# Loads issued further ahead of their use, and P1 of the next superblock between P5 and P3

## The chip, the cores and the metric

The kernel runs on one core of a Trainium2 chip. The metric is the device time of one execution in microseconds (us), less is better. Five engines work side by side, each through its own queue of instructions in order: PE (matmuls; its weight loads are shown as PEld), DVE (VectorE), ACT (ScalarE), POOL (GpSimd) and SP (SyncE, which here issues every DMA). An engine that waits for a semaphore holds up all that stands behind in its queue.

## What is computed

```python
def _attn_ref(q, k, v, g_norm):            # 8 batches, 8 heads, 576 tokens, head 64
    kv = np.einsum('bhsd,bhse->bhde', k, v)
    out = np.einsum('bhsd,bhde->bhse', q, kv)
    rms = np.sqrt(np.mean(out * out, axis=-1, keepdims=True) + 1e-06)
    return (out / rms * g_norm).astype(np.float32)

def _moe_ref(x, w_in, w_out):              # 4608 tokens, 512 -> 2048 -> 512
    h = x @ w_in
    g = np.maximum(0.01 * h, h)
    return (g @ w_out).astype(np.float32)

def _moe2_ref(x, w_in, w_out):             # the same sizes
    h = x @ w_in
    g = h - np.tanh(h)
    return (g @ w_out).astype(np.float32)

x = attention, heads side by side, one row for each of the 8 * 576 tokens
x = _moe_ref(x, moe_w_in, moe_w_out)
return _moe2_ref(x, moe2_w_in, moe2_w_out)
```

The weights of both layers come as 64-bit floats.

## The kernel before

**Products.** A matrix product is made by Strassen's scheme with seven products P1 to P7 of half-size blocks (the table `PROD`, the class `Blocks`). Each operand block is split into a high and a low fp16 part, and `three` (L483) makes three matmuls for each product of two blocks. The left or right operand comes in two tiles: `opa` holds the three blocks that are sums by themselves, `ops` four more. `left_stages` (L420) makes them: ACT writes the high part (L429, L431), DVE the low part (L436, L438), POOL and DVE make the sums (L468). The results of the products lie in PSUM banks: P1, P6 and P7 accumulate one after the other in bank a, P2 has b, P4 has d, P5 and then P3 have c. ACT copies bank a out (`c1` after P1, `u2` after P6, `u3` after P7: the tiles `c` and `u`, L523 to L527), and DVE adds those to the others (`add`, L531, L536 to L542): block 11 after P2, 21 after P7, 22 after P5, 12 after P3. Since P3 accumulates on bank c, it may only start when 22 has been added:

```python
            need = {6: "c1", 7: "u2", 3: "22"}.get(p)
```

**Stages.** (1) To about 105 us: attention of the first batch, conversion of the first weight. (2) up1, to 595 us: `up` makes h of the first layer in 8 superblocks (one batch each, T1 = 2 x 288 tokens), each of 8 units with seven products of 6 matmuls; an activation follows and the unit `g` goes to DRAM. Between the products stand the matmuls of the attention of the next batch (`between1`). (3) down1, to 942 us: `down` multiplies g by w_out, 8 superblocks of 336 matmuls; the result x (`xst`) goes to DRAM. (4) up2, to 1305 us: 9 superblocks of T2 = 2 x 256 tokens, with tanh. (5) down2, to the end: 9 superblocks.

**A superblock of up1.** Its x is the attention of one batch. When the norms of a batch are there, DVE takes the reciprocals (L856), SP stores them (`iv`, L859), SP loads them again spread over 64 partitions (`bc`, four loads for each half kk, L867), POOL multiplies (`xg`, L874), and `left_stages` makes the operands. All that has to be done before the first product of the next superblock. Meanwhile SP also issues the loads of k, v and q of later batches (L751), the words of weights to convert (L302), the units of converted weights to split (L390) and the stores of g (L606).

**A superblock of down.** `produce` loads the eight units of g (`gl`) and makes their operands, j = 0 to 7. `superblock` then runs P1, P2 (two token halves t each), P4 by j, P6, P7, P5, P3. Each product takes all eight units, 48 matmuls for both halves.

**What sets the order.** `Plan` is a list of events by planned time. Each step has a planned duration; a chain of steps gives (engine, duration, function) tuples, where an engine None with a duration is a lead: the function (a load) is called at once and the next step is planned so much later. PE's products follow each other by `plan.on_pe`, and `plan.pe` is the planned time of the next one. Events are written out in the order of planned times, and that is the order in each engine's queue on the chip. The planned times bind nothing else. The leads are:

```python
plan.chain(t, [(None, 4.5, load), (None, 0.0, room)] + stages + [(None, 0.0, store)])
more.append([(None, 5.0, lambda kk=kk: load(kk)), ("G", 2.7, lambda kk=kk: scale(kk))] + stages)
plan.chain(t + 3.5 * kk, [(None, 5.0, load)] + stages)
```

in this order: unit of a weight (`split_late`, L403), `bc` (L883), and x for a superblock of up2 (`x1g`, in `x1_operands`, L1111). `between2` calls `x1_operands` for the next superblock of up2, `start_t` calls it for superblock 0 in the last superblock of down1. The weights `w` of a layer are loaded whole (L415) as soon as the last superblock of the layer before has used the tile (`freed`).

**Places.** L, M and X are pools of 20, 11 and 13 tiles in SBUF (`Slots`): L the large ones (g, gl, bc, x1g, ops, words), M the tiles opa and unit, X the tiles c and u of `Blocks`.

Of the kernel before, what the change touches and what calls it, by code (L numbers as in the profile page):

```python
# [130 lines left out]
def body(ctx, tc, q, k, v, g_norm, w1, w2, w3, w4, out):  # L131
# [12 lines left out]
    NL, NM, NX = 20, 11, 13  # L144
# [237 lines left out]
    def split_late(n, i, kk, t, place):  # L382
# [20 lines left out]
        plan.chain(t, [(None, 4.5, load), (None, 0.0, room)] + stages + [(None, 0.0, store)])  # L403
# [236 lines left out]

    def down(blk, T, NS, mats, width, place, ready, start_of, freed, scales=None, scale=None):
# [34 lines left out]
        def superblock(s):  # L676
            t0 = plan.pe
            start_of(s, t0)
            if s + 1 < NS:
                produce(s + 1, t0 + 1.0)  # L680
            dur = mm(width)
            for t in range(2):
                sc = scales(s) if scales else (None, None)
                bk[s, t] = Blocks(
                    dict(a=t, b=2 + 3 * t, c=3 + 3 * t, d=4 + 3 * t), width, place(s, t), None, None, ready(s, t)
                )
                bk[s, t].now = {}
                if scales:
                    def late(s=s, t=t):
                        bk[s, t].scale, bk[s, t].minus = scales(s)  # L690
                    at(t0, late)

            def whole(p, t, js=range(NP)):
# [6 lines left out]
            early = range(NP - 2) if s == 0 else range(0)  # L700
            late = range(len(early), NP)
            for p in (1, 2):
                for t in range(2):
                    if early:
                        whole(p, t, early)
            for p in (1, 2):
                for t in range(2):
                    whole(p, t, late)
            for j in range(NP):
                for t in range(2):  # L710
                    e = whole(4, t, [j])
                give("A", j, e)
            for p in (6, 7):
                for t in range(2):
                    whole(p, t)
            for t in range(2):
                whole(5, t)
            for t in range(2):
                e = whole(3, t, range(2))
            for j in range(2):  # L720
# [3 lines left out]
            for j in range(2, NP):  # L724
                for t in range(2):
                    e = whole(3, t, [j])
                give("S", j, e)
                if s == NS - 1:
                    freed(j, e)
# [113 lines left out]
    def norms(b, e):  # L843
# [35 lines left out]
        for kk in range(2):  # L879
# [3 lines left out]
            more.append([(None, 5.0, lambda kk=kk: load(kk)), ("G", 2.7, lambda kk=kk: scale(kk))] + stages)  # L883
# [55 lines left out]
    def split_all():  # L939
        for n, (i, kk) in enumerate(UNITS):  # L940
            what = ("w", 0, i - 2, 1) if i >= 2 else "s_w1"
            when(what, plan.now + 0.3 + 2.5 * n, lambda i=i, kk=kk: plan.chain(plan.now, split_first(i, kk)))
# [28 lines left out]
    for (b, c), n0 in sorted(pos.items(), key=lambda x: x[1]):  # L971
# [6 lines left out]
        else:  # L978
            for (dur, fn, after), o in zip(pair(b, c, held), OFFS):
                extra.setdefault(n0 + o, []).append((dur, fn, after))  # L980
            loads.append((n0 - 9, b, c, held))
# [28 lines left out]

    spread(lambda i, kk, t: convert(1, i, kk, t, 6.0), UNITS, START + 52.0, START + 180.0)
    spread(lambda i, kk, t: split_late(1, i, kk, t, M), UNITS, START + 200.0, end1 - 60.0)
    spread(lambda i, kk, t: convert(2, i, kk, t, 6.0), UNITS, START + 182.0, end1 - 60.0)

# [80 lines left out]
    def x1_operands(s, t):  # L1095

        x1ops[s] = [{}, {}]
        for kk in range(2):
# [21 lines left out]
            plan.chain(t + 3.5 * kk, [(None, 5.0, load)] + stages)  # L1120
# [43 lines left out]
    spread(lambda i, kk, t: convert(3, i, kk, t, 6.0), UNITS, end2 - 45.0, c3)  # L1164
    e = c3 + 18.0
    scaled[3] = [lambda: [down_scales(state[x]) for x in ("whole", "rest")]]
    spread(lambda i, kk, t: split_late(3, i, kk, t, M), UNITS, e + 1.0, end3 - 55.0)
# [73 lines left out]
```

## Time and profile before

| | us |
|---|---|
| median of 3 runs (1645.23 to 1646.91) | 1646.12 |
| the profiled execution, whole | 1649.15 |
| its span in the profile | 1647.4 |
| PE busy | 1512.3 (92%) |
| DVE busy | 1301.6 (79%) |
| ACT busy | 867.2 (53%) |
| POOL busy | 746.0 (45%) |

The profile is of one execution, so differences are made against 1649.15, and the result is then compared with the median. Times in the trace count from the start of the span. A row of a timeline tells when a run of like instructions starts on an engine and how long it lasts, and in brackets how long the engine was idle before it and what ended that. PEclk is the granted TensorE clock as a share of full speed.

### The profile page before, as it was taken

To read this page: it belongs to the slowest core of one execution; us is meant where nothing else is said; L and a number is where in the kernel's file an instruction comes from. 1 tells how busy PE (TensorE), PEld (TensorE's weight loads), DVE (VectorE), ACT (ScalarE), POOL (GpSimd) and SP (SyncE) were. 2 spreads that over 40 slices of the span, in tenths; PEclk is the share of its full clock that TensorE was granted. 3 is DMA by queue.
4 is the path that set the end of the run, shared out by engine and by line. 5 is a ranking of instruction groups with operands and counts; after the bars stand their busy time and mean duration, and the time that the engine had idled before them with its cause. 6 is when DMAs were issued, how large, how long until landed. Compare 5 with 4: busy or idle time off the path is not lost. (4 is left out here: it accounts for less than half of the span.)

```text
span 1647.4 us, 32120 instructions
## 1 busy us (share of the span) xinstructions
PE 1512.3 (92%) x12274; PEld 1227.4 (75%) x12274; DVE 1301.6 (79%) x2113; ACT 867.2 (53%) x1381; POOL 746.0 (45%) x758
## 2 busy tenths in 40 slices
PE   5299898898989999999999979999999889999998
PEld 3156675666767777777777768888888778888887
DVE  4765676576667778889989669999999988888881
ACT  3366454465655664444444246666776645455441
POOL 0356203144143345666656134446887654444440
PEclk8589999999999999999999989999999999999999
DMA  9856897898896885545455565555666844444441
GB/s 210 172 88 160 227 239 208 245 245 235 252 259 209 282 318 168 185 145 200 155 172 173 184 233 206 186 210 196 243 240 243 316 143 143 157 129 135 145 132 33
DMA packets 251578, 322.08 MB, mean 196 GB/s; under 512 B 129440, under 2 KB 194080, under 8 KB 251424
## 3 DMA queue, kind: packets, MB, share of 16 engines
q1 hardware_dynamic: 251424, 320.03, 62.7%
q8 instruction: 96, 1.57, 0.4%
q14 instruction: 58, 0.48, 0.1%
HBM read 190.84 MB, written 129.12 MB: 194 GB/s over the span
## 5 line engine op out<-in xcount | busy, mean ns | idle before, releaser
L489 PEld LDWEIGHTS <-w 128*128 128x128 f16 x8400 | 824.8, 99 | 280.1 <-issue 98.7
L468 POOL TENSOR_TENSOR gl<-gl 128x256 f32<-128x256 f32 (+1 forms) x272 | 309.5, 1138 | 307.2 <-issue 79.9
L489 PE MATMUL ps_c<-ops,w 128*128 128x288 f16 (+1 forms) x2400 | 337.3, 285 | 40.2 <-DVE g L536 28.2
L489 PE MATMUL ps_a<-ops,w 128*128 128x288 f16 (+1 forms) x2400 | 333.6, 284 | 22.2 <-ACT u L527 10.3
L489 PEld LDWEIGHTS <-ops 128*128 128x128 f16 x1728 | 169.8, 98 | 28.8 <-issue 7.7
L372 POOL TENSOR_TENSOR unit<-unit 128x128 f32<-128x128 f32 x192 | 134.1, 699 | 116.0 <-DVE wo L365 97.4
L489 PE MATMUL ps_b<-opa,w 128*128 128x288 f16 (+1 forms) x1200 | 170.2, 287 | 0.0
L489 PE MATMUL ps_a<-opa,w 128*128 128x288 f16 (+1 forms) x1200 | 166.8, 283 | 2.9 <-DMA w<-wd 2.8
L489 PE MATMUL ps_d<-opa,w 128*128 128x288 f16 (+1 forms) x1200 | 165.9, 282 | 2.7 <-DVE g L536 2.7
L468 DVE TENSOR_TENSOR gl<-gl 128x256 f32<-128x256 f32 (+1 forms) x272 | 156.0, 576 | 3.3
L874 POOL TENSOR_TENSOR xg<-xg,bc 128x1152 f32<-128x1152 f32 x16 | 43.1, 2694 | 254.3 <-DMA bc<-iv 208.7
L1145 POOL TENSOR_TENSOR g<-g,th 128x512 f32<-128x512 f32 x72 | 101.0, 1403 | 95.9 <-ACT th L1142 95.7
L431 ACT ACTIVATE ops<-gl,inv 128x1024 f16<-128x1024 f32 x72 | 82.6, 1147 | 110.2 <-POOL gl L468 102.9
L489 PEld LDWEIGHTS <-opa 128*128 128x128 f16 x1296 | 126.8, 98 | 16.6 <-issue 1.9
L429 ACT ACTIVATE ops<-gl 128x1152 f16<-128x1152 f32 x64 | 74.3, 1162 | 99.5 <-POOL gl L468 94.6
L438 DVE SCALAR_TENSOR_TENSOR ops<-gl,inv,ops 128x1024 f16<-128x1024 f32 x72 | 104.4, 1451 | 15.8 <-ACT ops L431 15.4
L436 DVE TENSOR_TENSOR ops<-gl,ops 128x1152 f16<-128x1152 f32 x64 | 99.8, 1559 | 19.9 <-ACT ops L429 19.7
L365 DVE SCALAR_TENSOR_TENSOR wo<-unit,s_w,wo 128x384 f16<-128x384 f32 (+1 forms) x96 | 83.4, 871 | 27.1 <-ACT wo L362 26.7
L489 PE MATMUL ps_c<-w,ops 128*128 128x256 f16 x864 | 98.4, 275 | 3.8 <-DVE osb L536 3.8
L489 PE MATMUL ps_a<-w,ops 128*128 128x256 f16 x864 | 96.1, 273 | 3.2 <-ACT u L527 3.2
L468 POOL TENSOR_TENSOR x1g<-x1g 128x256 f32<-128x256 f32 x72 | 68.1, 946 | 65.1 <-DMA x1g<-x 34.7
L438 DVE SCALAR_TENSOR_TENSOR opa<-gl,inv,opa 128x768 f16<-128x768 f32 x72 | 87.2, 1211 | 12.5 <-ACT opa L431 12.5
(118 smaller groups left out, 2192.3 us busy)
## 6 DMA issues: line engine op xcount, KB each, us to landing
g<-g SPq DMA_DIRECT2D x64, 576.0 KB, 4.4
gl<-g SPq DMA_DIRECT2D x64, 576.0 KB, 4.7
g<-g SPq DMA_DIRECT2D x72, 512.0 KB, 3.0
gl<-g SPq DMA_DIRECT2D x72, 512.0 KB, 4.5
wd<-wo SPq DMA_DIRECT2D x48, 448.0 KB, 2.8
w<-wd SPq DMA_DIRECT2D x24, 896.0 KB, 7.4
words<-in_moe_w_in_dram SPq DMA_DIRECT2D x64, 256.0 KB, 5.0
words<-in_moe_w_out_dram SPq DMA_DIRECT2D x64, 256.0 KB, 4.0
```

The source lines that it names most:

```text
L365: nc.vector.scalar_tensor_tensor(out=dst()[:, 1, a:b], in0=cols(0, n), scalar=scale(), in1=dst()[:, 0, a:b], op0=ALU.mult, op1=ALU.subtract,)
L372: nc.gpsimd.tensor_tensor(out=o, in0=a, in1=b, op=ALU.subtract)
L429: nc.scalar.activation(out=o, in_=i_, func=AF.Copy)
L431: nc.scalar.activation(out=o, in_=i_, func=AF.Identity, scale=scale())
L436: nc.vector.tensor_tensor(out=o, in0=i_, in1=h, op=ALU.subtract)
L438: nc.vector.scalar_tensor_tensor(out=o, in0=i_, scalar=scale(), in1=h, op0=ALU.mult, op1=ALU.subtract)
L468: lambda: e.tensor_tensor(out=g()[:, o], in0=g()[:, a], in1=g()[:, b], op=op),
L489: nc.tensor.matmul(out=out_, lhsT=a, rhs=c, start=start and m == 0, stop=stop and m == n - 1, skip_group_check=not fresh,)
L874: nc.gpsimd.tensor_tensor(out=x, in0=x, in1=held[kk].ap, op=ALU.mult)
L1145: e.tensor_tensor(out=g()[:, n], in0=g()[:, n], in1=held["t"].ap[:, n], op=ALU.subtract)
```

## The change

Six things change; the computation stays.

1. **Leads in up1.** Unit of a weight 4.5 to 9.0, words (`convert`) 6 to 13 with the start 7 earlier, `bc` 5 to 6; the loads of k, v and q stand four places earlier among the products (`n0 - 13`); conversion and splitting of late weights end 15 earlier.
2. **x of up2.** Lead of `x1g` 5 to 10; the call in `between2` at 12 before the planned PE time in place of 1 after, that in `start_t` 15 earlier.
3. **`down`.** P2 and P4 take turns by j; P1 of the next superblock stands between P5 and P3 and takes its two halves in turn; `produce` is called 6.8 (`AHEAD`) before P2 in place of 1.0 after the start of P1. Superblock 0 has P1 and P2 at its start, as before.
4. **Pools.** L 20 to 22, X 13 to 8.
5. **split_all** starts its units in pairs.
6. **split_late of the last weight** takes its tiles from L in place of M.

```diff
@@ pools @@
-    NL, NM, NX = 20, 11, 13
+    NL, NM, NX = 22, 11, 8
@@ split_late @@
-        plan.chain(t, [(None, 4.5, load), (None, 0.0, room)] + stages + [(None, 0.0, store)])
+        plan.chain(t, [(None, 9.0, load), (None, 0.0, room)] + stages + [(None, 0.0, store)])
@@ down @@
-        def superblock(s):
-            t0 = plan.pe
-            start_of(s, t0)
-            if s + 1 < NS:
-                produce(s + 1, t0 + 1.0)
-            dur = mm(width)
+        dur = mm(width)
+        one = 2 * NP * 3 * dur
+
+        def blocks(s):
...
-            for p in (1, 2):
-                for t in range(2):
-                    whole(p, t, late)
-            for j in range(NP):
-                for t in range(2):
-                    e = whole(4, t, [j])
-                give("A", j, e)
-            for p in (6, 7):
+            def in_turn(ps, s=s, then=None):
+                for j in range(NP):
+                    for p in ps:
+                        for t in range(2):
+                            e = whole(p, t, [j], s)
+                    if then:
+                        then(j, e)
+
+            start_of(s, plan.pe)
+            if s == 0:
+                blocks(0)
+                for js in (range(NP - 2), range(NP - 2, NP)):
+                    for p in (1, 2):
+                        for t in range(2):
+                            whole(p, t, js)
+            if s + 1 < NS:
+                produce(s + 1, plan.pe - AHEAD - (one if s == 0 else 0.0))
+            in_turn((4,) if s == 0 else (2, 4), then=lambda j, e: give("A", j, e))
+            for p in (6, 7, 5):
                 for t in range(2):
                     whole(p, t)
-            for t in range(2):
-                whole(5, t)
-            for t in range(2):
-                e = whole(3, t, range(2))
...
+            if s + 1 < NS:
+                blocks(s + 1)
+                in_turn((1,), s + 1)
...
+            in_turn((3,), then=end)
@@ operands of up1, attention, weights @@
-            more.append([(None, 5.0, lambda kk=kk: load(kk)), ("G", 2.7, lambda kk=kk: scale(kk))] + stages)
+            more.append([(None, 6.0, lambda kk=kk: load(kk)), ("G", 2.7, lambda kk=kk: scale(kk))] + stages)
-            loads.append((n0 - 9, b, c, held))
+            loads.append((n0 - 13, b, c, held))
-    spread(lambda i, kk, t: convert(1, i, kk, t, 6.0), UNITS, START + 52.0, START + 180.0)
-    spread(lambda i, kk, t: split_late(1, i, kk, t, M), UNITS, START + 200.0, end1 - 60.0)
-    spread(lambda i, kk, t: convert(2, i, kk, t, 6.0), UNITS, START + 182.0, end1 - 60.0)
+    spread(lambda i, kk, t: convert(1, i, kk, t, 13.0), UNITS, START + 45.0, START + 173.0)
+    spread(lambda i, kk, t: split_late(1, i, kk, t, M), UNITS, START + 200.0, end1 - 75.0)
+    spread(lambda i, kk, t: convert(2, i, kk, t, 13.0), UNITS, START + 175.0, end1 - 75.0)
@@ x of up2 @@
-            plan.chain(t + 3.5 * kk, [(None, 5.0, load)] + stages)
+            plan.chain(t + 3.5 * kk, [(None, 10.0, load)] + stages)
-            state["whole"] = second_scales(0, whole, t0 + 9.0)
-            x1_operands(0, t0 + 17.0)
+            state["whole"] = second_scales(0, whole, t0 + 5.0)
+            x1_operands(0, t0 + 2.0)
-            x1_operands(n // (NOP * NP) + 1, plan.pe + 1.0)
+            x1_operands(n // (NOP * NP) + 1, plan.pe - 12.0)
```

How this moves instructions, at three places. On SP, around the store of the norms of the fifth batch (`iv_73`) in up1, before:

```order
L606 DMA g_2_6_131<-g 128x1152
L347 DMA wf_0_0_261<-unit 128x512
L751 DMA k<-in_k_dram 96x6x64 x2
L751 DMA v<-in_v_dram 96x6x64 x2
L751 DMA q<-in_q_dram 96x6x64 x2
L302 DMA words<-in_moe_w_in_dram 128x2x256 x2
L859 DMA iv_73<-iv 16x288
L606 DMA g_2_7_132<-g 128x1152
L867 DMA bc<-iv_73 64x2x288 x4
L390 DMA unit<-wf_0_0_245 128x512
L867 DMA bc<-iv_73 64x2x288 x4
```

The same stretch in the changed kernel:

```order
L302 DMA words<-in_moe_w_in_dram 128x2x256 x2
L606 DMA g_2_6_131<-g 128x1152
L754 DMA k<-in_k_dram 96x6x64 x2
L754 DMA v<-in_v_dram 96x6x64 x2
L754 DMA q<-in_q_dram 96x6x64 x2
L347 DMA wf_0_0_261<-unit 128x512
L862 DMA iv_73<-iv 16x288
L606 DMA g_2_7_132<-g 128x1152
L870 DMA bc<-iv_73 64x2x288 x4
L390 DMA unit<-wf_0_0_245 128x512
L870 DMA bc<-iv_73 64x2x288 x4
```

The loads of k, v and q, and one pair of words, no longer stand right ahead of `iv_73` but further up, with a store of `wf` between; the `bc` loads stand behind it as they did.

On DVE, in the third superblock of down1, from the subtraction in block 21 of the second half (`xst<-u`, `ps_d`) to what follows the two adds of block 22 (`xst<-ps_c`; `u_8110` and `u_8149` are the first and the second half of the tokens), before:

```order
L540 TENSOR_TENSOR xst<-u_8149,ps_d 128x288
L894 TENSOR_REDUCE mx_322<-xst 128x1
L468 TENSOR_TENSOR gl<-gl 128x288
L894 TENSOR_REDUCE mx_322<-xst 128x1
L468 TENSOR_TENSOR gl<-gl 128x288
L542 TENSOR_TENSOR xst<-ps_c,u_8110 128x288
L436 TENSOR_TENSOR ops<-gl,ops 128x1152
L436 TENSOR_TENSOR opa<-gl,opa 128x864
L542 TENSOR_TENSOR xst<-ps_c,u_8149 128x288
L365 SCALAR_TENSOR_TENSOR wo<-unit,s_w_5985,wo 128x384
```

The same stretch in the changed kernel:

```order
L540 TENSOR_TENSOR xst<-u_8153,ps_d 128x288
L436 TENSOR_TENSOR ops<-gl,ops 128x1152
L468 TENSOR_TENSOR gl<-gl 128x288
L542 TENSOR_TENSOR xst<-ps_c,u_8112 128x288
L365 SCALAR_TENSOR_TENSOR wo<-unit,s_w_5923,wo 128x512
L436 TENSOR_TENSOR opa<-gl,opa 128x864
L897 TENSOR_REDUCE mx_322<-xst 128x1
L542 TENSOR_TENSOR xst<-ps_c,u_8153 128x288
L897 TENSOR_REDUCE mx_322<-xst 128x1
L468 TENSOR_TENSOR gl<-gl 128x288
```

Between the two adds stand a weight split, an operand split and a maximum, where there were two operand splits. On PE the 48 matmuls of P1 stand between those of P5 and P3 now.

On SP, at the start of up2, the loads of x for its second superblock (`x1g`) and of the weights (`w`), before:

```order
L415 DMA w_3_10819<-wd_3_304 128x3584
L415 DMA w_4_10829<-wd_4_305 128x3584
L415 DMA w_5_10838<-wd_5_306 128x3584
L415 DMA w_6_10846<-wd_6_307 128x3584
L415 DMA w_7_10873<-wd_7_308 128x3584
L1111 DMA x1g<-x_0_0_77 128x64
L1111 DMA x1g<-x_0_1_78 128x448
```

The same stretch in the changed kernel:

```order
L1118 DMA x1g<-x_0_0_77 128x64
L1118 DMA x1g<-x_0_1_78 128x448
L1118 DMA x1g<-x_2_0_93 128x64
L1118 DMA x1g<-x_2_1_94 128x448
L302 DMA words<-in_moe_w_out_dram 128x2x256 x2
L1042 DMA x_1_7_92<-xst 128x288
L1118 DMA x1g<-x_1_0_85 128x64
L1118 DMA x1g<-x_1_1_86 128x448
L1118 DMA x1g<-x_3_0_101 128x64
L1118 DMA x1g<-x_3_1_102 128x448
L1042 DMA x_2_7_100<-xst 128x288
L415 DMA w_0_10800<-wd_0_301 128x3584
```

The eight `x1g` loads have moved from behind the eight `w` loads to ahead of them, in two groups around the store of `x_1_7`.

## Rows read from the trace of the kernel before

**Rows 1.** Windows by stage: length, busy PE PEld DVE ACT POOL (instructions), PEclk, DMA share, GB/s.

```profile
105.30:594.80 489.50, 454.47 (x3362) 336.50 (x3361) 331.25 (x640) 278.95 (x533) 160.52 (x185) 0.96 0.80 232
594.80:942.00 347.20, 331.76 (x2654) 261.40 (x2652) 302.08 (x429) 156.58 (x203) 195.87 (x185) 0.99 0.53 177
...
975.00:1305.00 330.00, 320.30 (x2898) 283.18 (x2897) 317.81 (x531) 225.76 (x360) 208.79 (x206) 1.00 0.64 225
...
1349.00:1647.40 298.40, 294.23 (x2690) 262.78 (x2687) 230.95 (x293) 132.65 (x160) 119.98 (x114) 1.00 0.40 125
```

**Rows 2.** Timeline, fourth stop of up1: start, duration, instruction, [idle before, releaser].

```profile
308.30 1.34 DVE L856 RECIPROCAL iv<-iv 16x96 f32<-16x96 f32 x2
...
313.74 0.53 SPq L859 DMA_DIRECT2D iv<-iv  x1
...
317.40 2.58 SPq L867 DMA_DIRECT2D bc<-iv  x4
...
320.66 2.52 SPq L867 DMA_DIRECT2D bc<-iv  x4
...
326.81 2.69 POOL L874 TENSOR_TENSOR xg<-xg,bc 128x1152 f32<-128x1152 f32 x1 [0.53 <-DVE wo L365]
...
331.10 1.60 PE L489 MATMUL ps_c<-ops,w 128*128 128x288 f16 x6 [4.54 <-DVE g L536]
```

**Rows 3.** Timeline of ACT, second stop of up1.

```profile
194.56 0.67 ACT L314 ACTIVATE unit<-words 128x512 f32<-128x512 f32 x1 [8.20 <-DMA words<-in_moe_w_out_dram]
```

**Rows 4.** Down1: waits of PE and DVE (total, times, longest), windows, timelines.

```profile
PE ps_c L489 <- DVE xst L542: 11.9, 8, 2.8
...
DVE ops L436 <- ACT ops L429: 12.8, 13, 1.9
...
636.45:678.90 42.45, 41.31 (x338) 32.87 (x336) 38.94 (x53) 21.01 (x27) 27.35 (x25) 1.00 0.53 174
...
sum 262.91, PE 251.42 PEld 198.60 DVE 238.99 ACT 124.90 POOL 164.59; mean PE 41.90 PEld 33.10 DVE 39.83 ACT 20.82 POOL 27.43
...
676.35 1.05 DVE L436 TENSOR_TENSOR opa<-gl,opa 128x864 f16<-128x864 f32 x1
...
715.74 1.64 DVE L436 TENSOR_TENSOR opa<-gl,opa 128x864 f16<-128x864 f32 x1
...
717.80 6.98 PE L489 MATMUL ps_c<-ops,w 128*128 128x288 f16 x42 [2.72 <-DVE xst L542]
```

**Rows 5.** Windows of 10 us behind two stops, columns as in rows 1.

```profile
717.80:727.80 10.00, 10.00 (x68) 7.34 (x68) 8.16 (x14) 3.42 (x5) 5.30 (x6) 0.83 0.59 204
...
961.80:971.80 10.00, 9.97 (x66) 7.85 (x66) 7.60 (x23) 6.90 (x10) 4.64 (x5) 0.71 0.16 47
```

**Rows 6.** Timeline of SP, ACT and PE, start of up2.

```profile
931.11 0.33 SPq L1035 DMA_DIRECT2D x<-xst  x1
...
938.52 3.85 SPq L415 DMA_DIRECT2D w<-wd  x6
944.26 5.28 SPq L1111 DMA_DIRECT2D x1g<-x  x4
...
960.48 0.93 ACT L431 ACTIVATE opa<-x1g,s_x 128x768 f16<-128x768 f32 x1 [12.82 <-DMA x1g<-x]
...
961.83 1.44 PE L489 MATMUL ps_a<-ops,w 128*128 128x256 f16 x6 [10.33 <-ACT u L527]
```

**Rows 7.** Timeline of PE and DVE, start of down2.

```profile
1342.73 6.41 PE L489 MATMUL ps_c<-w,ops 128*128 128x256 f16 x42 [2.86 <-DVE osb L536]
1348.98 5.40 PE L489 MATMUL ps_a<-w,opa 128*128 128x256 f16 x48
...
1349.98 1.01 DVE L438 SCALAR_TENSOR_TENSOR opa<-gl,inv,opa 128x768 f16<-128x768 f32 x1
```

**Rows 8.** DMA issues: count, KB each, median us from issue to landing.

```profile
bc<-iv SPq DMA_DIRECT2D x64, 144.0 KB, 4.4
...
iv<-iv SPq DMA_DIRECT2D x8, 18.0 KB, 3.4
```

More of the change, by code (lines that the diff above doesn't have):

```diff
@@ L638, in up @@
                 count += 1
+    AHEAD = 6.8
     def down(blk, T, NS, mats, width, place, ready, start_of, freed, scales=None, scale=None):
@@ L674, in work_ @@
             return plan.on_pe(3 * len(js) * dur, go)
-        def superblock(s):
-            t0 = plan.pe
-            start_of(s, t0)
-            if s + 1 < NS:
-                produce(s + 1, t0 + 1.0)
-            dur = mm(width)
+        dur = mm(width)
+        one = 2 * NP * 3 * dur
+        def blocks(s):
             for t in range(2):
-                sc = scales(s) if scales else (None, None)
                 bk[s, t] = Blocks(
@@ L690, in late, with superblock, whole @@
                         bk[s, t].scale, bk[s, t].minus = scales(s)
-                    at(t0, late)
-            def whole(p, t, js=range(NP)):
+                    at(plan.pe, late)
+        def superblock(s):
+            def whole(p, t, js=range(NP), s=s):
                 e = work_(s, p, t, js, dur)
@@ L698, in give, with end @@
                 at(e, lambda: (M if kind == "A" else L).give(ops[s, j][kind]))
-            early = range(NP - 2) if s == 0 else range(0)
-            late = range(len(early), NP)
-            for p in (1, 2):
-                for t in range(2):
-                    if early:
-                        whole(p, t, early)
-            for p in (1, 2):
-                for t in range(2):
-                    whole(p, t, late)
-            for j in range(NP):
-                for t in range(2):
-                    e = whole(4, t, [j])
-                give("A", j, e)
-            for p in (6, 7):
+            def in_turn(ps, s=s, then=None):
[16 more added lines that the diff above has]
+            for p in (6, 7, 5):
                 for t in range(2):
                     whole(p, t)
-            for t in range(2):
-                whole(5, t)
-            for t in range(2):
-                e = whole(3, t, range(2))
-            for j in range(2):
+            if s + 1 < NS:
+                blocks(s + 1)
+                in_turn((1,), s + 1)
+            def end(j, e):
                 give("S", j, e)
@@ L723, in superblock @@
                     freed(j, e)
[L724 to L729, printed above, removed]
+            in_turn((3,), then=end)
         return produce, superblock, span
@@ L939, in split_all, with pair_ @@
     def split_all():
-        for n, (i, kk) in enumerate(UNITS):
+        def pair_(i):
+            for kk in range(2):
+                plan.chain(plan.now + 2.5 * kk, split_first(i, kk))
+        for i in range(NP):
             what = ("w", 0, i - 2, 1) if i >= 2 else "s_w1"
-            when(what, plan.now + 0.3 + 2.5 * n, lambda i=i, kk=kk: plan.chain(plan.now, split_first(i, kk)))
+            when(what, plan.now + 0.3 + 5.0 * i, lambda i=i: pair_(i))
     scaled[0] = [split_all]
@@ L1163, in body @@
     c3 = end2 + 0.45 * (end3 - end2)
-    spread(lambda i, kk, t: convert(3, i, kk, t, 6.0), UNITS, end2 - 45.0, c3)
+    spread(lambda i, kk, t: convert(3, i, kk, t, 13.0), UNITS, end2 - 45.0, c3)
     e = c3 + 18.0
     scaled[3] = [lambda: [down_scales(state[x]) for x in ("whole", "rest")]]
-    spread(lambda i, kk, t: split_late(3, i, kk, t, M), UNITS, e + 1.0, end3 - 55.0)
+    spread(lambda i, kk, t: split_late(3, i, kk, t, L), UNITS, e + 1.0, end3 - 55.0)
     out_view = out.rearrange("(b p c) d -> b c p d", p=CP, c=NC)
```

## The prediction

> **What bounds the kernel now.** I read the stages first [rows 1]. PE is the engine that is nearly always busy: 454.47 of 489.50 us in the first up stage (up1), 331.76 of 347.20 in the first down stage (down1), 320.30 of 330.00 in the bulk of up2, 294.23 of 298.40 in the bulk of down2. What a change can win without taking away matmuls is therefore PE's idle time and the time that PE runs at the lower clock. In up1 that is 489.50 - 454.47 = 35.0 us idle, and a mean granted clock of 0.96, which over 454 us of busy time is about 0.04 x 454 = 18 us. In down1 it is 15.4 us idle at 0.99. In bulk down2 it is 4.2 us, in bulk up2 9.7 us, and there DVE is busy for 317.81 of 330.00 us, so DVE is the second bound.
>
> Then I looked for what ends the idle times, one stage at a time.
>
> In up1 PE stops about once in each superblock. At the fourth stop [rows 2] the chain reads backwards like this: PE waits 4.54 us at 331.10 for a block that DVE writes; DVE and ACT stand behind the splitting of the next x operand; that waits for POOL's scaling `xg`, whose second half starts at 326.81; POOL waits for the broadcast `bc`, whose loads SP issues at 317.40 and 320.66; these need the stored norms `iv`, issued at 313.74, though the last reciprocal was done at 308.30 + 1.34 = 309.64. Four us of that are lost on SP, behind the loads of k, v and q (and one pair of words), which the order of SP before shows right ahead of the `iv` store. A second kind of stop is that ACT itself waits in its queue for a load: 8.20 us for the words of a weight at 194.56 [rows 3].
>
> In down1 PE waits eight times, 11.9 us in all, for the DVE add `xst` between P5 and P3 [rows 4]: P3 accumulates into the bank that P5 filled, and DVE has to add from it first. At 717.80 this costs 2.72 us; DVE was held by an operand split, 1.64 us at 715.74. After it the clock is 0.83 for 10 us [rows 5], 1.7 us more.
>
> At the start of up2 PE waits 10.33 us at 961.83 [rows 6]: ACT, which keeps the banks of the first superblock, stands in its queue behind the split of the second superblock's operand, and that waits 12.82 us for `x1g`, whose loads SP issues at 944.26, behind six weight loads at 938.52. At the start of down2 one wait of 2.86 us at 1342.73 [rows 7] is again P5 to P3.
>
> **Part 1, loads of up1: 24 us saved.** The stop at each superblock is set by how late the second half of `xg` starts. The code plans it 1.8 + 3.0 + 5.0 = 9.8 us after the last reciprocal, and 10.8 with the new lead of 6. In [rows 2] it came at 326.81 - 309.64 = 17.2, so 7.4 late. The change moves k, v and q four places up, out of the stretch between reciprocal and store, so the 4 us on SP go. What is left is a chain that no lead shortens, since it starts at the reciprocal: `iv` issue 0.53 and landing 3.4, four `bc` issues 2.58, a unit load 0.59, three quarters of the next 2.52, and 4.4 until the last has landed (medians of landing in [rows 8]). The sum is 0.5 + 3.4 + 2.6 + 0.6 + 1.9 + 4.4 = 13.4, still 2.6 after the plan. I take 2.5 us of stop for each of six superblocks, 15, and 4 us for what has other causes: 19 us idle in place of 35, 16 saved. A stop of that size costs 1.7 us of clock (the nearest in size is that of 2.72 us in down1, with 0.83 for 10 us after it, [rows 4, 5]), six of them 10 in place of 18: 8 saved. Together 24. The words and units, loaded 7 and 4.5 us earlier, cover ACT's 8.20 of [rows 3], which is inside the 16. The ends: if transfers stay as late as now, because the queue is as full with other loads, only ACT's wait goes, 6 us; if the chain no longer holds PE, 31 idle and 16 of clock go, 47. If earlier loads only push `bc` back further, 6 us are lost, which is the worst that I count.
>
> The Trainium skill, "SBUF — State Buffer", section "The DMA setup-cost knee", gives a transfer some 2 us plus its bytes at 436 GB/s. That is an estimate of 2.0 us for the 18 KB of `iv` and 2.3 for 144 KB; the trace has 3.4 and 4.4. With the page's figures the chain would be 9.9 and there would be no stop, which is the second case below.
>
> **Part 2, the order in down1: 12 us saved.** The matmuls are the same ones. P1 of the next superblock (48 matmuls, 5.9 us at 41.3 us of PE for 336, [rows 4]) now lies between P5 and P3, so that DVE has 5.9 us more for the add. The longest wait was 2.8, so all eight go: 11.9, and 2 x 1.7 of clock after the two longest, 15.3 at most. What is late next is the eighth operand of P1. Before, at 678.90, it was written at 676.35 + 1.05 = 677.40, and PE asked for it 7/8 x 2.9 us into P1, at 681.5: 4.1 us to spare. Now P1 stands 5.9 us earlier, but takes both halves in turn, so that its eighth part comes 5.1 us in: 3.3 earlier than before. The operands are begun 6.8 us before P2 where it was 1.0 after the start of P1, that is 1.9 earlier. So 4.1 - 3.3 + 1.9 = 2.7 us are left. The other end is DVE. In six superblocks of 262.91 us together it is busy for 238.99 and waits 12.8 for ACT's halves [rows 4], so it needs up to (239.0 + 12.8) / 6 = 42.0 us each, against 43.8 now and 41.3 of PE. If those waits stay, DVE sets the superblock, and seven of them give 7 x 1.8 = 12.6. I take 12. The upper end is the 15; for the lower, one split more in each superblock that takes 1.64 in place of 1.05 us [rows 4] leaves 7 x 1.2 = 8, and I go to 7.
>
> **Part 3, start of up2: 12 us saved.** These loads of `x1g` are now planned 13 us earlier (12 before the superblock in place of 1 after its start), and on SP it stands ahead of all weight loads, its last loads just behind the store of `x_1_7`, which was issued at 931.11. So it comes some 944.3 - 932 = 12 us earlier, and the 10.33 us of PE go; the clock after it (0.71 for 10 us, [rows 5]) gives 2.9: 13.2 at most. I keep back 1 for the weights, which now stand behind those 5.28 us of issues, while P1 of the first unit needs the first of them. Lower bound 6, if the 5.28 and its clock, 7 in all, come back.
>
> **Part 4, start of down2: 0.** The 2.86 us of [rows 7] and 1.7 of clock go, 4.6. But here the eighth operand of the next P1 was written at 1349.98 + 1.01 = 1350.99, with P1 at 1348.98 asking for it 2.3 us in, 0.3 to spare. P1 now comes 5.3 earlier for the order (48 matmuls in 5.4 us with the last one's end, [rows 7]) and 2.9 for the removed wait, and asks 2.3 later within itself: 5.9 earlier, for operands that are begun 2.6 earlier, with 0.3 to spare. A new wait of up to 3.0, with 1.7 of clock, takes the place: 4.7 lost for 4.6 won, so 0, between -4 and +4 for a DVE that is that much ahead or behind.
>
> **Part 5, the rest: 0.** Bulk down2 has PE busy for all but 4.2 us [rows 1]; there the new order finds nothing to fill. Bulk up2 is held by DVE, and its own operands, begun 13 us earlier, change nothing for DVE. Eight places for intermediates instead of thirteen could make ACT wait for an add; no row shows that. One late tile in each of 16 superblocks, by one DVE split of 1.64 us [rows 4], would be 26; I take 0, because a superblock's intermediates come free at many operations and not at one, and let the upper end of the range hold some of it. Two more places in L take nothing.
>
> **Sum.** 24 + 12 + 12 + 0 + 0 = 48 us. The profiled execution took 1649.15 us, of which the span is 1647.4; it is 3.0 over the median of 1646.12. From the median: 1646.1 - 48 = 1598.
>
> **The rivals.** *The chain of norms vanishes.* If landings in the loosened queue are as short as their best, part 1 is 47: 47 + 12 + 12 = 71, so 1575. For it: the DMA share of 0.80 in up1 [rows 1] includes what is now moved. Against: moving loads forward takes no byte out.
>
> *The queue stays as it is, and DVE holds down1.* Part 1 gives 6, part 2 gives 8, part 3 gives 12: 26, so 1620. For it: the DMA share of 0.80 over the whole stage, and DVE at 302.08 of 347.20 us in down1 [rows 1]. The second half of this has a shown cause: the same split takes 1.05 us at 676.35 and 1.64 us at 715.74 [rows 4]. The Trainium skill, "SBUF — State Buffer", section "Who interferes with whom", says that a DVE instruction with two SBUF inputs contends with a GpSimd instruction that reads SBUF; if POOL's work moves against DVE's, DVE would be the bound in all of down1.
>
> *Slower: the early P1 waits for its own operands.* P1 crosses over in 7 places of down1 and 8 of down2. With only 2.7 us to spare in the one and less than none at the first of the other, a DVE that comes 5.2 us later than before would make PE wait 2.5 at each, plus 1.7 for the clock: 15 x 4.2 = 63 us. With parts 1 and 3 standing, 36, that is 27 more than before, 1673. It decides where a crossing costs 36 / 15 = 2.4 us, a wait of 0.7 with its 1.7 of clock, which is a DVE 3.4 us later than before. Against: DVE is not slower for the change, and works on the same amount between two P1.
>
> *Nothing moves,* 1646: SP's queue might be bound by the transfers' completion, so that issuing earlier only waits earlier, and PE's stops in down1 shift to P1. For both at once I see no row.
>
> **Numbers.** Forecast 1598 (1587 to 1609): 0.50. Chain vanishes, 1575: 0.18. Queue and DVE hold, 1620: 0.20. Nothing, 1646: 0.04. Slower, 1673: 0.08. Leaving out the last two and the outer half of what spreads around 1575 and 1620 gives 1572 to 1628. A measurement of this kernel can tell about 0.2% (3.3 us) from no change. Faster 0.88, same 0.04, slower 0.08.
>
> **What would show it.** Part 1: in up1 the `iv` store follows the last reciprocal within 1 us, PE's idle time is near 19 us and the remaining stops, of 2 to 3 us, are still released through `xg` and `bc`; wrong if POOL's waits for `bc` are gone with PE's stops, or if `bc` is as late as before. Part 2: no PE wait for `xst` in down1, superblocks of 41.3 to 42.5 us; wrong if PE waits at P1 for `opa`. Part 3: no wait over 2 us at the first unit of up2. Part 4: a PE wait for `opa` in the first P1 that crosses in down2. The forecast fails as a whole if up1's stops have another cause than these loads.

## The result

The changed kernel takes 1607.38 us (median, 1606.39 to 1610.44), the kernel before in the same comparison 1646.51. The ratio is 0.9765, with a 95% interval of 0.9748 to 0.9782. The forecast was 1598, with a range of 1572 to 1628. The time lies 9 us above the forecast and inside the range.

To see where the time went, both traces are cut at the first matmul of each stage. (The cut between up1 and down1 lies 4.7 us earlier here than in [rows 1], at down1's first matmul, and down2 begins at its own.) The windows of the kernel before, columns as in [rows 1]:

```profile
0.00:105.32 105.32, 54.34 (x207) 35.32 (x208) 66.52 (x137) 40.25 (x85) 31.18 (x46) 0.69 0.81 167
105.32:590.05 484.73, 449.70 (x3324) 332.69 (x3323) 326.67 (x635) 275.06 (x529) 157.27 (x183) 0.96 0.80 231
590.05:942.03 351.98, 336.51 (x2693) 265.22 (x2691) 306.70 (x434) 160.45 (x207) 199.10 (x186) 0.99 0.54 180
942.03:1301.12 359.09, 338.38 (x3031) 297.66 (x3032) 330.50 (x572) 234.93 (x376) 212.21 (x210) 0.98 0.65 230
1301.12:1647.40 346.28, 333.40 (x3026) 296.49 (x3023) 271.25 (x339) 156.54 (x188) 146.23 (x135) 0.99 0.43 135
```

And of the changed kernel:

```profile
0.00:98.52 98.52, 52.89 (x207) 33.55 (x208) 65.37 (x137) 40.22 (x85) 30.91 (x47) 0.72 0.96 188
98.52:560.29 461.77, 440.10 (x3323) 327.41 (x3322) 334.18 (x635) 275.44 (x529) 159.26 (x183) 0.99 0.81 240
560.29:902.68 342.39, 331.75 (x2693) 262.99 (x2691) 307.31 (x431) 160.19 (x207) 199.86 (x186) 1.00 0.55 187
902.68:1264.26 361.58, 337.75 (x3031) 297.05 (x3031) 334.69 (x574) 233.81 (x375) 210.49 (x210) 0.99 0.63 227
1264.26:1605.30 341.04, 333.48 (x3025) 296.41 (x3023) 275.14 (x339) 153.35 (x188) 145.11 (x135) 1.00 0.43 137
```

| stage | before | changed | difference | forecast |
|---|---|---|---|---|
| start | 105.3 | 98.5 | -6.8 | 0 |
| up1 | 484.7 | 461.8 | -23.0 | -24 |
| down1 | 352.0 | 342.4 | -9.6 | -12 |
| up2 | 359.1 | 361.6 | +2.5 | -12 |
| down2 | 346.3 | 341.0 | -5.2 | 0 |
| span | 1647.4 | 1605.3 | -42.1 | -48 |

The two profiled executions differ by 42.1 us, the medians by 39.1, because the profiled one of the kernel before lies 3 us over its median. The sum came out nearly right, but one stage is wrong by 14.5 us and two are wrong the other way.

**up1** behaves as forecast on the face of it. PE's idle time (length less busy) is 21.7 us, where 19 were forecast, and the clock is 0.99 where it was 0.96. What is left of the stop of [rows 2]: lines of DVE, SP, POOL and PE in the changed kernel.

```profile
288.64 1.34 DVE L859 RECIPROCAL iv<-iv 16x96 f32<-16x96 f32 x2
...
290.05 0.82 SPq L862 DMA_DIRECT2D iv<-iv  x1
...
293.45 2.59 SPq L870 DMA_DIRECT2D bc<-iv  x4
...
296.72 2.53 SPq L870 DMA_DIRECT2D bc<-iv  x4
...
304.36 2.80 POOL L877 TENSOR_TENSOR xg<-xg,bc 128x1152 f32<-128x1152 f32 x1 [1.12 <-DMA bc<-iv]
...
308.14 1.08 PE L489 MATMUL ps_c<-ops,w 128*128 128x288 f16 x4 [3.69 <-DVE g L536]
```

The last reciprocal ends at 289.98 and the store is issued at 290.05, where it was 4.1 us late before. The second half of `xg` starts 14.4 us after the reciprocal (17.2 before, 13.4 forecast). This batch is one of the better ones. Read in the same way, the five batches in the middle of up1 (the third to the seventh of eight) take 15.9 us on the average, 14.4 to 17.3, where it was 17.3 before, 16.6 to 19.0. The `iv` store follows the reciprocal within 0.6 us in seven batches of eight, and 2.4 us late in one; before it was 3.2 to 4.1 us late in three.

The waits of ACT in up1 (total, times, longest) tell something that the forecast had not weighed. Before:

```profile
ACT wo L362 <- DMA unit<-wf: 22.4, 3, 8.8
ACT opa L429 <- POOL xg L874: 14.3, 10, 3.5
ACT unit L314 <- DMA words<-in_moe_w_out_dram: 13.6, 3, 8.2
...
ACT unit L314 <- DMA words<-in_moe_w_in_dram: 8.0, 6, 2.4
```

Changed kernel:

```profile
ACT opa L429 <- POOL xg L877: 28.0, 12, 5.2
...
ACT sq L813 <- DMA iv<-iv: 4.4, 3, 2.8
```

The 44 us that ACT waited for words and units of the weights are gone, and its wait for `xg` has doubled. Two late things had stood in ACT's queue.

**down1.** The waits of PE, against [rows 4]:

```profile
PE ps_a L489 <- ACT u L523: 4.2, 3, 2.9
PE ps_a L489 <- DVE opa L436: 2.9, 3, 1.4
PE ps_a L489 <- DMA w<-wd: 2.7, 1, 2.7
PE pt L222 <- DVE mx L1066: 0.7, 1, 0.7
PE ps_c L489 <- DVE xst L542: 0.2, 1, 0.2
```

The 11.9 us for `xst` are 0.2 now. What takes their place is 4.2 us for ACT's copy between P6 and P7, and 2.9 us at P1 for its own operands. So PE's idle time falls only by 4.8 us (15.5 to 10.6); its busy time falls by as much, with the clock at 1.00 in place of 0.99.

**up2.** The first superblock is 7.0 us shorter, the fifth 5.7 us longer: the windows of these two in the changed kernel.

```profile
902.68:947.68 45.00, 38.21 (x340) 33.02 (x340) 36.98 (x77) 22.94 (x38) 14.70 (x14) 1.00 0.77 284
1061.58:1104.58 43.00, 39.16 (x341) 33.91 (x339) 36.23 (x66) 23.68 (x40) 19.47 (x20) 0.96 0.44 155
```

The same two before:

```profile
942.03:994.03 52.00, 40.55 (x339) 34.49 (x340) 34.60 (x78) 24.18 (x40) 15.96 (x14) 0.87 0.65 242
1107.33:1144.63 37.30, 37.30 (x342) 33.27 (x341) 34.01 (x66) 23.77 (x40) 21.72 (x22) 1.00 0.52 180
```

At the start of up2 the wait of [rows 6] has another owner now. SP, ACT and PE of the changed kernel:

```profile
901.43 3.82 SPq L415 DMA_DIRECT2D w<-wd  x4
907.45 0.83 SPq L1042 DMA_DIRECT2D x<-xst  x2
...
920.66 0.47 ACT L527 ACTIVATE u<-ps_a,up 128x256 f32<-128x256 f32 x1 [4.85 <-DMA x<-xst]
...
921.19 0.82 PE L489 MATMUL ps_a<-ops,w 128*128 128x256 f16 x6 [2.29 <-ACT u L527]
```

ACT has no place in X for `u` until the store of x issued at 907.45 has landed, 13.1 us later, at 920.58: it was issued behind the weights (8 x 896 KB), the last of which landed at 920.17.

### The profile page after: what moved, and what is told of

Read it like the earlier page. It is cut to its first block, busy times and chain, and to the rows that moved or that the text cites. A ratio compares the mean times of both kernels' runs of the same rounds, so it can differ in the third digit from the quotient of the medians.

```text
span 1605.3 us, 32279 instructions
## 1 busy us (share of the span) xinstructions
PE 1496.0 (93%) x12274; PEld 1217.4 (76%) x12274; DVE 1316.7 (82%) x2113; ACT 863.0 (54%) x1381; POOL 745.6 (46%) x758
## 5 line engine op out<-in xcount | busy, mean ns | idle before, releaser
L489 PE MATMUL ps_c<-ops,w 128*128 128x288 f16 (+1 forms) x2400 | 331.3, 282 | 33.1 <-DVE g L536 32.8
L489 PE MATMUL ps_d<-opa,w 128*128 128x288 f16 (+1 forms) x1200 | 172.9, 281 | 3.4 <-DVE g L536 3.3
L489 PE MATMUL ps_b<-opa,w 128*128 128x288 f16 (+1 forms) x1200 | 174.6, 283 | 0.0
L468 DVE TENSOR_TENSOR gl<-gl 128x256 f32<-128x256 f32 (+1 forms) x272 | 162.9, 604 | 3.7
L536 DVE SCALAR_TENSOR_TENSOR g<-ps_c,u 128x288 f32<-128x288 f32 x128 | 57.8, 452 | 50.6 <-PE ps_c L489 50.4
L527 ACT ACTIVATE u<-ps_a,up 128x256 f32<-128x256 f32 x144 | 68.0, 472 | 50.8 <-PE ps_a L489 45.5
```

The costliest lines, as they stand in the source:

```text
L468: lambda: e.tensor_tensor(out=g()[:, o], in0=g()[:, a], in1=g()[:, b], op=op),
L489: nc.tensor.matmul(out=out_, lhsT=a, rhs=c, start=start and m == 0, stop=stop and m == n - 1, skip_group_check=not fresh,)
L527: nc.scalar.activation(out=t, in_=src, func=AF.Identity, scale=self.scale)
L536: nc.vector.scalar_tensor_tensor(out=o, in0=src, scalar=self.minus if sub else self.scale, in1=t, op0=ALU.mult, op1=ALU.add,)
```

## The experiments

Each is timed in rounds against the kernel before on the same chip, so that the ratios can be set beside the 0.9765 of the changed kernel. Stage lengths are of the profiled execution, cut as above.

**What held up1.** The loads of the chain alone put back, in the changed kernel (e1):

```diff
-            more.append([(None, 6.0, lambda kk=kk: load(kk))
+            more.append([(None, 5.0, lambda kk=kk: load(kk))
-            loads.append((n0 - 13, b, c, held))
+            loads.append((n0 - 9, b, c, held))
```

> The changed kernel, but with the loads of k, v, q and the lead of bc as before (n0 - 9, 5.0). Theory A (the forecast: up1 is held by the chain norms, iv, bc, xg, and the 23 us that up1 lost came from its shortening): the iv store stands behind k, v, q again, up to 4 us late, PE's idle time in up1 goes from 21.7 back to 30 or more, and the time to some 1623 us (+16). Theory B (up1 was held by ACT waiting in its queue for words and units of the weights, and the chain alone holds little): up1 stays within 5 us of its 461.8, time 1607 to 1612.

Ratio 0.9872 (0.9848 to 0.9896), 1627.37 us. up1 is 480.0 us, only 4.7 shorter than the 484.7 of the kernel before. (The lead of `bc` and the places of k, v and q were not put back one by one; e8 and e12 below move each of them further.) Then the loads for the weights alone put back (the splitting of the second weight keeps its earlier end; e2):

```diff
-        plan.chain(t, [(None, 9.0, load), (None, 0.0, room)] + stages + [(None, 0.0, store)])
+        plan.chain(t, [(None, 4.5, load), (None, 0.0, room)] + stages + [(None, 0.0, store)])
-    spread(lambda i, kk, t: convert(1, i, kk, t, 13.0), UNITS, START + 45.0, START + 173.0)
+    spread(lambda i, kk, t: convert(1, i, kk, t, 6.0), UNITS, START + 52.0, START + 180.0)
-    spread(lambda i, kk, t: convert(2, i, kk, t, 13.0), UNITS, START + 175.0, end1 - 75.0)
+    spread(lambda i, kk, t: convert(2, i, kk, t, 6.0), UNITS, START + 182.0, end1 - 60.0)
```

> The changed kernel, but with the leads of words and of units, and the places of their conversions, as before (6.0 and 4.5). Theory A: only ACT's waits for words come back, some 6 us, 1613. Theory B: ACT's waits for words and units (44 us in up1 before, none after) come back and with them PE's stops, 15 to 20 us in up1, 1622 to 1627.

Ratio 0.9869 (0.9841 to 0.9897), 1627.23 us. up1 is 484.6 us: nothing is won in it. So the first run agrees with theory A and the second with theory B, and neither theory stands as it was put. The waits of ACT in up1 show why. The chain put back:

```profile
ACT opa L429 <- POOL xg L877: 39.6, 12, 5.8
...
ACT sq L813 <- DMA iv<-iv: 10.3, 3, 7.1
```

The weights' loads put back:

```profile
ACT wo L362 <- DMA unit<-wf: 30.3, 9, 7.2
ACT unit L314 <- DMA words<-in_moe_w_out_dram: 20.1, 9, 7.2
ACT unit L314 <- DMA words<-in_moe_w_in_dram: 16.8, 7, 3.8
ACT opa L429 <- POOL xg L877: 11.9, 6, 5.1
```

With one of the two put back, ACT waits longer for that one, and PE stops about as long as before (31.6 and 34.8 us idle, 35.0 before). This fits two late things in parallel, where PE's time follows the later one; it is argued from these totals and not followed stop by stop. Nor are the two quite separate. From the last reciprocal to the second half of `xg`, in the mean of the same five batches, it is 15.9 us in the changed kernel, 16.8 with the chain's loads put back and 17.2 with the weights' loads put back: these lengthen the chain as well. The 23 us come only when both are moved, and can't be divided between them: undone singly they are worth 18 and 23.

**How much lead the chain wants.** The changed kernel with a planned lead of 9 for `bc` (e8):

```diff
-            more.append([(None, 6.0, lambda kk=kk: load(kk))
+            more.append([(None, 9.0, lambda kk=kk: load(kk))
```

> The changed kernel with a planned lead of 9 us for bc in place of 6, nearer to what the chain of norms takes (14 to 17 us against 10.8 planned). If what PE waits for in up1 is work that stands behind the late step in the queues of ACT and DVE: the step is planned where it can run, PE's idle time in up1 falls from 21.6 to 12 to 17, and the time to 1599 to 1603. If PE waits for the operands of the superblock themselves, nothing is won: 1606 to 1610.

Ratio 0.9704 (0.9676 to 0.9732), 1597.34 us, faster than the changed kernel. up1 is 455.2 us, with PE idle for 17.2. Loads are issued no earlier by this; the late step is only planned later, so that less stands behind it. The chain itself is no shorter (16.8 us in the mean of the five batches, 15.9 in the changed kernel), and still ACT's wait for `xg` falls from 28.0 to 17.4 us. PE's largest waits in up1 are these, where the first was 15.5 in the changed kernel:

```profile
PE ps_c L489 <- DVE g L536: 6.9, 8, 1.6
PE ps_a L489 <- ACT u L525: 4.7, 2, 3.9
PE ps_d L489 <- DVE g L536: 2.1, 2, 1.7
```

**The order in the down stages.** The new order alone, on the kernel before (`down` as in the change, pools of 22 and 8, and the first x of up2 begun at t0 + 7; e3):

```diff
-    NL, NM, NX = 20, 11, 13
+    NL, NM, NX = 22, 11, 8
-            state["whole"] = second_scales(0, whole, t0 + 9.0)
-            x1_operands(0, t0 + 17.0)
+            state["whole"] = second_scales(0, whole, t0 + 5.0)
+            x1_operands(0, t0 + 7.0)
```

> The kernel before with the new order of the down stages alone (and the pools of 22 and 8 tiles that it needs, and the first x of up2 begun 10 us earlier, without which the order can't be written). If the gain of the down stages is the order's own: down1 and down2 shorten by 9.6 and 5.2 us, no wait for xst, about 1631. If the eight tiles of X or P1's own operands cost: waits of ACT for a tile or of PE for opa, and 1633 to 1640. If the loads were what helped there: 1640 to 1646.

Ratio 0.9922 (0.9899 to 0.9945), 1635.19 us. down1 is 8.9 and down2 5.1 us shorter than before, 14.0 of the 14.8 that they lost in the changed kernel, and the waits in down1 are nearly the same: 0.2 for `xst`, 3.4 for ACT's copy, 2.5 for `opa` at P1. The other way round, the changed kernel with the old `down` (e4):

```diff
-            for p in (6, 7, 5):
+            for p in (6, 7):
                 for t in range(2):
                     whole(p, t)
-            if s + 1 < NS:
-                blocks(s + 1)
-                in_turn((1,), s + 1)
+            for t in range(2):
+                whole(5, t)
...
```

> The changed kernel with the old order of the down stages. The waits for xst come back (11.9 us before, with clock 15), down1 352 and down2 346 us as before: 1607 + 15 = 1622. If the new order had no part in it, it stays at 1607 to 1612.

Ratio 0.9826 (0.9799 to 0.9854), 1620.72 us. The wait is back, in down1:

```profile
PE ps_c L489 <- DVE xst L542: 11.5, 6, 2.9
```

Down1 is 349.6 and down2 344.1 us long, 7.2 and 3.1 more than in the changed kernel. So 10 to 14 of the 14.8 us are the order's own.

**Places in X.** The kernel before with eight in place of thirteen (e5):

```diff
-    NL, NM, NX = 20, 11, 13
+    NL, NM, NX = 20, 11, 8
```

> The kernel before with eight places in X in place of thirteen, nothing else. If places cost what the trace of the changed kernel shows (ACT waits 4.9 us for the last store of x before it may write u, and 4.4 us for the store of iv before sq): 4 to 8 us longer than before, 1650 to 1655, with ACT waits for stores that before has nowhere. If they cost nothing, as the forecast took it: 1645 to 1648.

Ratio 1.0006 (0.9990 to 1.0023): no difference that can be told. Some waits for stores are there, though:

```profile
ACT sq L810 <- DMA iv<-iv: 11.8, 4, 5.8
...
ACT u L525 <- DMA iv<-iv: 3.1, 1, 3.1
...
ACT c L523 <- DMA x<-xst: 1.4, 1, 1.4
```

X holds more than the tiles c and u: also qt, sq and iv of the attention and the results `xst` and `osb`, and iv and the results come free only when their stores have landed. That in this kernel these waits lie inside longer ones is argued, not shown. In the changed kernel they count: with nine places and the lead of 9 (e10),

```diff
-    NL, NM, NX = 22, 11, 8
+    NL, NM, NX = 22, 11, 9
```

> The lead of 9 us for bc with nine places in X in place of eight. If one place more frees ACT from the stores of iv and x (5.3 and 4.9 us of waiting with eight): up1 and up2 2 to 3 us shorter each, 1592 to 1595. If those waits are covered: 1596 to 1599.

the ratio is 0.9645 (0.9614 to 0.9675), 1591.41 us, against 0.9704 without the place. The first superblock of up2 takes 40.8 us in place of 45.0, and ACT waits 1.5 us for the store of x where it was 4.9, though that store takes 13.4 us to land. up1 is no shorter for the place (455.5 us against 455.2), and up2 is 2.0 shorter (357.5 against 359.5). The two profiled executions differ by 2.1 us and the medians by 5.9, so how much the place brings in all is known only as 2 to 6.

**The start of up2.** Only the loads of x for up2 earlier, on the kernel before (with the pools of 22 and 8 and the last `split_late` in L; e6):

```diff
-            plan.chain(t + 3.5 * kk, [(None, 5.0, load)] + stages)
+            plan.chain(t + 3.5 * kk, [(None, 10.0, load)] + stages)
-            x1_operands(n // (NOP * NP) + 1, plan.pe + 1.0)
+            x1_operands(n // (NOP * NP) + 1, plan.pe - 12.0)
```

> The kernel before with only the loads of x in up2 earlier (between2 12 us ahead, lead 10, and the pools 22 and 8 with the last split_late in L, which it needs to be written). Theory of the forecast: the 10.3 us stop at the start goes and the stage is 12 shorter, 1634 to 1636. Rival from the changed kernel's trace: the first superblock gains 7 to 10, but DVE has the same work in the stage and gives back part of it later, so up2 is 0 to 6 us shorter, 1640 to 1648.

Ratio 1.0008 (0.9993 to 1.0022): nothing. up2 is 362.6 us long, no shorter than the 359.1 before. PE still stops for 5.95 us at the first superblock, and now ACT stands behind the words of a weight:

```profile
961.65 0.66 ACT L314 ACTIVATE unit<-words 128x512 f32<-128x512 f32 x1 [7.16 <-DMA words<-in_moe_w_out_dram]
```

The change also gave the words of the last weight a lead of 13 in place of 6; these are loaded at the same planned time as before and converted 7 us later. The changed kernel with that put back (e7) shows the same wait:

```diff
-    spread(lambda i, kk, t: convert(3, i, kk, t, 13.0), UNITS, end2 - 45.0, c3)
+    spread(lambda i, kk, t: convert(3, i, kk, t, 6.0), UNITS, end2 - 45.0, c3)
```

> The changed kernel with the words of the last weight loaded 6 us ahead as before, in place of 13. If the loss in the fifth superblock of up2 (43.0 us against 37.3 before, with the search for the weight's largest value falling among the operand splits) comes from that shift: up2 some 5 us shorter, 1602. If DVE's load in the stage as a whole holds it, the loss only goes elsewhere: 1606 to 1609.

Ratio 0.9790 (0.9765 to 0.9815), 1611.92 us. The fifth superblock falls from 43.0 to 38.6 us, so the shift of the last weight's conversion does make that loss. But the first rises from 45.0 to 48.4 and the next three from about 38.0 to 38.6, and up2 is 362.0 us long, against 361.6 in the changed kernel. At the start ACT waits again for words:

```profile
924.70 0.66 ACT L314 ACTIVATE unit<-words 128x512 f32<-128x512 f32 x1 [7.93 <-DMA words<-in_moe_w_out_dram]
```

So in four kernels ACT waits for three different things there, x, a store of x, and (twice) words, and what they share is to be issued behind the weights. The test is to spread these out, in the changed kernel (e9):

```diff
-        return lambda i, e: at(e + 0.2, lambda: load_weights(n, i))
+        return lambda i, e: at(e + 0.2 + (2.2 * i if n == 2 else 0.0), lambda: load_weights(n, i))
```

> The changed kernel with the eight weight loads of up2 (7.3 MB, which land one after the other from 902.6 to 920.2 us in the changed kernel) issued 2.2 us further apart each. If it is their bytes that hold up what SP issues behind them (the last stores of x took 13.1 us to land, and ACT waited 4.9 us for a place that such a store holds): the store lands in 2 to 5 us, ACT's wait and the PE stop of 2.3 us go, the first superblock of up2 takes 41 to 43 us in place of 45.0. If the weights then come late for their own units: PE waits for w. If DVE sets the stage, what the first superblock wins is lost later: total 1604 to 1608; otherwise 1602 to 1604.

Ratio 0.9727 (0.9709 to 0.9745), 1603.39 us. The store of x lands in 6.3 us (2 to 5 were expected), ACT has no wait for it, and the first superblock is down to 40.8 us with the same work, at a DMA share of 0.87 in place of 0.77:

```profile
904.63:945.43 40.80, 38.13 (x340) 33.01 (x341) 36.41 (x76) 23.25 (x39) 14.16 (x14) 1.00 0.87 313
```

up2 is 356.0 us, 5.6 less than in the changed kernel, so the 4.2 of the first superblock stay. The rest lies in the fifth, which takes either 41.4 or 43.0 us in kernels with the same code there.

**Together.** Lead 9, nine places and spread weights, the three diffs above in one kernel (e11):

> Lead of 9 us for bc, nine places in X and the spread weight loads together. If the three act in different places, the gains add: 1590 to 1594. If DVE sets up2: 1594 to 1597.

Ratio 0.9677 (0.9655 to 0.9699), 1594.60 us, not to be told from the 0.9645 without the spreading. The gains do not add: the ninth place and the spreading remove the same wait, and the first superblock is 40.8 us with either or both. Then also the loads of k, v and q four places further ahead (e12):

```diff
-            loads.append((n0 - 13, b, c, held))
+            loads.append((n0 - 17, b, c, held))
```

> The same, with the loads of k, v and q four more places earlier (n0 - 17). If what still delays the iv store by 3.3 to 3.6 us in two superblocks of up1 is these loads: up1 3 to 6 us shorter. If it is other loads, or if more lead only moves the collision: within 2 us of the kernel without it, or longer.

Ratio 0.9628 (0.9605 to 0.9651), 1586.43 us, the lowest median here (its interval overlaps that of the 0.9645): 3.7% under the kernel before, where the change is 2.35%. up1 is 446.3 us at a clock of 1.00, 6.0 less than without the last step, with PE idle for 11.9. Here the chain is shorter, 14.5 us in the mean of the five batches against 16.2 without the last step:

```profile
99.38:545.65 446.27, 434.36 (x3323) 325.52 (x3322) 333.12 (x636) 274.38 (x529) 158.56 (x185) 1.00 0.85 249
```

## Why the prediction was right, and where not

**Part 1, 24 forecast, 23.0 measured.** The size was right: PE's idle time fell by 13.4 us (16 forecast), its busy time by 9.6 with the higher clock (8 forecast). The division was not. The text let the chain of norms set the stop at each superblock, put ACT's wait for loads inside the 16, and took 6 us for the case that it alone goes ("only ACT's wait goes, 6 us"). But the chain's loads moved by themselves are worth nothing (e2: 484.6 us), and the weights' loads by themselves 4.7 (e1). The two act together, and the lower end of 6 would have been about right, and even too high, for a change that had moved only one. The row of ACT's 8.20 us [rows 3] showed the second; its total, 44 us in ACT's waits, was not looked at. The chain that was left was priced too low: one stop stood for six, and 13.4 forecast against 15.9 measured in the mean. "A chain that no lead shortens" was beside the point: a larger planned lead for `bc` shortens not the chain but what waits behind it, 6.6 us in up1 (e8). It was not quite true either, since k, v and q moved further ahead do shorten it (e12).

**Part 2, 12 forecast, 9.6 measured.** All waits for `xst` went, as said. The term that was mis-sized is what comes next: the forecast had DVE set the superblock at 42.0 us, 1.8 less than before. From P2 to the next P2 the seven spacings average 43.0 us where they were 44.4 before, 1.4 less, and PE's new waits are 4.2 us for ACT's copies and 2.9 for operands at P1. The rival "the early P1 waits for its own operands" is real, but with 2.9 us in down1 it has less than a tenth of its 63.

**Part 3, 12 forecast, -2.5 measured.** This step failed, twice. "The 10.33 us of PE go", it said, and "I keep back 1 for the weights": the weights did not hold up PE, but the next thing behind them did, the store of x. This is also where part 5 is wrong, which took 0 for the eight places: it saw the intermediates alone, while X holds the results until their stores have landed; one more place or looser weights bring 4.2 us in this superblock (e10, e9). And the gain of 7.0 in the first superblock was given back by a loss of 5.7 in the fifth and smaller ones after it. There the change places the search for the last weight's largest value among DVE's splits (before it lies in the same superblock, but earlier, at 1112.14, and PE does not stop there at all). Lines of DVE and PE in the changed kernel:

```profile
1071.87 1.23 DVE L258 SCALAR_TENSOR_TENSOR m_w<-m_w,t_w 128x1 int32<-128x1 int32 x1
...
1073.24 0.27 PE L222 MATMUL pt<-ident,m_w 128*1 128x128 f32 x1 [1.70 <-DVE m_w L258]
...
1081.97 0.82 PE L489 MATMUL ps_c<-ops,w 128*128 128x256 f16 x6 [2.15 <-DVE g L536]
```

Most of the 1.23 us of the first line is a wait for POOL, as the last section shows. Two stops of 1.70 and 2.15 us and the 1.9 us that PE is busy longer, at a clock of 0.96, are the 5.7. Part 5 had called bulk up2 "held by DVE" and left it at that; what was missing there is that moving work on DVE (conversion 7 us later, operands 13 earlier) is not free in a stage in which it is busy for 92% of the time. That the whole stage could not win is not so: e9 has 3.1 us less in up2 than the kernel before.

**Part 4, 0 forecast, -5.2 measured.** The term that was mis-sized is DVE's lead. The last operand of the first P1 that crosses was thought to come 2.6 us earlier. DVE and PE in the changed kernel:

```profile
1299.05 5.49 PE L489 MATMUL ps_a<-w,opa 128*128 128x256 f16 x48
...
1302.85 1.01 DVE L438 SCALAR_TENSOR_TENSOR opa<-gl,inv,opa 128x768 f16<-128x768 f32 x1
```

It is written 1303.86 - 1264.26 = 39.6 us into the stage, where it was 1350.99 - 1301.12 = 49.9 before [rows 7]: 10.3 earlier, of which the forecast had 2.6. DVE, which was idle for 7.6 of the first 47.9 us, is idle for 0.7 of the first 47.7 now; that the rest comes from this is argued. P1 runs through in 5.49 us, against 5.40 without a wait. The slack counted from planned times left out that DVE had time to spare.

**The start, 0 forecast, -6.8 measured.** Not settled. Over the profiled executions of ten kernels with the new start it is 98.1 to 102.8 us long, over four with the old one 101.0 to 105.3. Some 2 to 3 us may be the change's; the rest is in the spread from one execution to another. It was not tried by itself.

In all: up1 came out as forecast, down1 a little less, and the 14.5 us that up2 fell short of its forecast are nearly made up by 12.0 that down2 and the start gave unasked. That the time lay so near is in part luck: without these 12.0 it would have been some 1619, where the text had the rival in which the queue and DVE hold (1620).

## What to carry to other kernels

When an in-order queue waits for several late things, add up each thing's waits on that queue before dividing a gain between them: removing one exposes the other, and only both together pay. When a burst of large loads goes out, ask not only what is ahead of it now but what stands behind it then, stores that hold buffers among them. A step that is known to be late is worth planning late, with its real latency, even where nothing about the step itself can be made faster.

## What the runs showed of the hardware

A store of 144 KB that took 2.8 us to land in the median before took 13.1 us when it was issued behind eight loads of 896 KB, and words issued behind such loads made ACT wait 7 to 8 us (e6, e7): what was issued behind the weights landed behind them, the store 0.4 us after the last load. With the loads spread out it took 6.3 us (e9).

On DVE the operation on 128x1 integers at 1071.87 lasted 1.23 us, while POOL ran this:

```profile
1071.82 1.26 POOL L1152 TENSOR_TENSOR g<-g,th 128x512 f32<-128x512 f32 x1 [1.40 <-ACT th L1149]
```

In the kernel before the same operation stands where POOL is idle:

```profile
1112.14 0.16 DVE L258 SCALAR_TENSOR_TENSOR m_w<-m_w,t_w 128x1 int32<-128x1 int32 x1
```

Over all fourteen traces it was held 22 times, always while POOL ran an operation on two operands; it then lasted 0.57 to 2.62 us and ended 0.01 to 0.02 us after POOL's. Everywhere else it took 0.16 us. The Trainium skill, "SBUF — State Buffer", section "Who interferes with whom", says that a DVE instruction with two SBUF inputs contends with a GpSimd instruction that reads SBUF, and calls the port pair that they share an exclusive lock. The rows agree: an operation of 0.16 us became one of 1.23, held until POOL's had ended.
